# Agent attention with a squared-ReLU feed-forward: four transposes per group in one set, values weighed a block ahead over seven groups, second weights decoded in two parts

## The chip, the core and the metric

The kernel runs on one core of one Trainium2 chip. The time is the device time of one execution in microseconds (us). Three executions of the kernel before took 1960.69, 1955.43 and 1959.62 us; the median is 1959.62.

The engines are named as the profile names them: PE is the matrix engine (PEld its weight loads), DVE the vector engine, ACT the scalar (activation) engine, POOL the GpSimd engine, SP the engine that issues the DMAs.

## The reference

```python
B, N, C = 4, 12480, 128; n_agents = 49; d_ff = 2048
def sm(a, b):                         # softmax over the last axis
    s = (a @ b.transpose(0, 2, 1)) / sqrt(C); s = s - s.max(-1, keepdims=True)
    e = exp(s); return e / (e.sum(-1, keepdims=True) + 1e-9)
x = sm(q, agents) @ (sm(agents, k) @ v)        # 4 x 12480 x 128
h = maximum(x.reshape(-1, 128) @ w_in, 0)      # w_in 128 x 2048, as 64-bit floats
return (h * h) @ w_out                         # w_out 2048 x 128, as 64-bit floats
```

All is float32 but the two weight matrices, which arrive as 64-bit floats and are decoded on the chip from their two 32-bit words (`raw[:, :, 0]` low, `raw[:, :, 1]` high).

## The kernel before

**Tokens.** A group is 960 tokens (eight tiles of 120), so each of the four batches has 13 groups and there are 52. A group has two halves of 480 tokens and 16 slots; half 0 has slots 0 to 7, half 1 slots 8 to 15. A slot covers 256 of the 2048 hidden columns for one half. The loop works in pairs of slots (8 pairs a group): `first` issues the products into `h` for both slots, `second` the products into `o` for the slots four earlier (`LAG = 4`, so two pairs earlier). `o` is one PSUM bank; it is summed over a half's eight slots and then scaled out of PSUM by DVE as `ob` (`out`). With the lag, the sum of half 0 begins in the third pair of its group (slot 4) and that of half 1 in the seventh (slot 12); in each of these places the first product into `o` must wait until DVE has read the sum before.

**One pair.** PE: four products `h<-w,aw_hi`, four short ones `h<-x,aw_ex` side by side, then twelve into `o`. ACT: `r` twice (ReLU) and `g_hi` (the square, 1920 columns). DVE: `gg`, `h` (in place in PSUM) and `g_lo`. POOL: two `g_lo`. `gg` has two buffers (`GB`), `h` three, `g_lo` four.

**Attention beside it.** While batch b is fed forward, a generator (`background`) makes the attention of batch b+1: 13 blocks of `scores` (keys), `maxima`, 13 blocks of `values`, then `tables`, which makes `aw_hi` and `aw_ex`, the product of the attention with `w_in`. `step` advances it to its next `yield`, whose number is a price in slots; a `yield 0` stands ahead of a product and is passed only in the slots of `SPOTS`. Products of this kind go to one PSUM bank (`psa`), and `share` puts them between the first products of `o`: as a rule eight in a slot, four where `many` is set. Where a sum into `o` begins, some may stand ahead of its first product.

**Queries.** For each group, `queries` makes the scores of its 960 tokens (8 products), the softmax, transposes of its weights (4 in all), and, by 28 small DMAs over SP, the tiles `w` and `x` of both halves. It too is advanced at fixed slots: DMA of `qt` in slot 4 two groups ahead, scores in slot 14 (half of them put in slot 14, half in slot 0), softmax in slots 1 to 3, two transposes in slot 8, two in slot 12.

**Prologue.** Before group 0 the attention of batch 0 runs alone (13 key blocks, 13 value blocks, `tables`) with the decode of `w_in`. `w_out` is loaded in eight chunks (`load_w_out`) and decoded in group 0, behind the first `aw_half` (`issue_after(state[0]["cut"])`): the eight maxima, a power of two, then eight times `decode_w_out`.

**Order.** The instructions are put into each engine's queue by a scheduler; `queued` and `issue_after` fix that one comes behind another on its engine. An engine takes its queue in order.

Of the kernel before, what the change touches and what calls it, by code (L numbers as in the profile page):

```python
# [18 lines left out]
P = 128  # L19
# [16 lines left out]
PAIRED = (0, 2, 1, 3, 4, 6, 5, 7)  # L36
SPOTS = (1, 2, 3, 5)
# [3 lines left out]
def agent_attention_relu2(ctx: ExitStack, tc: tile.TileContext, qT, kT, v, agT, w_in, w_out, outT):  # L41
# [54 lines left out]
    def decoded(raw, up=None):  # L96
        low, high = raw[:, :, 0], raw[:, :, 1]
# [7 lines left out]
        nc.vector.tensor_scalar(t, t, 0x07FFFFFF, 3, op0=ALU.bitwise_and, op1=ALU.logical_shift_left)  # L105
        nc.vector.scalar_tensor_tensor(
            out=t, in0=high, scalar=0xC0000000, in1=t, op0=ALU.bitwise_and, op1=ALU.bitwise_or
        )
        if up is not None:
            nc.vector.tensor_scalar_mul(t.bitcast(F32), t.bitcast(F32), up)  # L110
# [3 lines left out]
        nc.vector.scalar_tensor_tensor(out=rest, in0=low, scalar=2.0**-52, in1=rest, op0=ALU.mult, op1=ALU.mult)  # L114
        return t.bitcast(F32), rest

    def load_w_in(dec, n):
        cs = slice(n * WCH, (n + 1) * WCH)
        t, rest = decoded(load_raw(w_in.bitcast(U32)[:, 2 * n * WCH : 2 * (n + 1) * WCH]))
        nc.gpsimd.tensor_add(win[:, cs], t, rest)  # L120
        nc.vector.reduce_max(top[:, n : n + 1], win[:, cs], axis=AX.X, apply_absolute_value=True)
# [10 lines left out]
    def powers_of_w_out():  # L132
# [11 lines left out]
        queued(nc.tensor.matmul, nc.tensor, ps[:, :1], ones, e.bitcast(F32), start=True, stop=True)  # L144
# [55 lines left out]
    def scores(b, i, kt):  # L200
# [7 lines left out]
        yield 1.2  # L208
# [29 lines left out]
    def halves(out, x, n, eng):  # L238

        nc.scalar.copy(out[:, :, :n], x)  # L240
        yield 1
        last[eng] = eng.tensor_sub(out[:, :, n:], x, out[:, :, :n].bitcast(F32))

    def values(b, i, vt, whole, eng):
# [6 lines left out]
        if not whole:  # L251
# [4 lines left out]
            yield 1  # L256
# [5 lines left out]
        yield 1  # L262
# [3 lines left out]
        else:  # L266
            e = small.tile([TP, NT, R], F32R, name="e2", bufs=2)
            yield from halves(e, d, NA, eng)
            vt = vs
        yield 0  # L270
# [9 lines left out]
        if i == 0 and not whole:  # L280
            nc.vector.tensor_copy(st["av"], pv[:R, :W])
        else:
            nc.vector.tensor_add(st["av"][:R, :W], st["av"][:R, :W], pv[:R, :W])

    def tables(b):
# [3 lines left out]
        nc.vector.tensor_add(x, st["av"][:, : C + 1], st["av"][:, C + 1 :])  # L289
# [68 lines left out]
    def queries(g, early=None):  # L358
# [29 lines left out]
        pairs = e.rearrange("p (j u h) a -> p j u (h a)", j=2, h=2)  # L388
        for j in range(2):
            yield  # L390
            pt = bank()
            w = qp.tile([P, G], F32R, name=f"w{j}", bufs=2)
            x = qp.tile([P, G], F16, name=f"x{j}", bufs=2)
            weights[g].append((w, x))
            if early:
# [10 lines left out]
                for t in range(NQ):  # L406
                    nc.sync.dma_start(x[t * 32 : t * 32 + NL, :], half[SP:, :])
                continue
            put([
                product(  # L410
                    pt[:K2, u * TP : (u + 1) * TP], pairs[:, j, u], ident[:TP, :TP],
                    is_transpose=True, start=True, stop=True,
                )
                for u in range(2)
            ])
            yield
            y = qp.tile([K2, 2 * TP], F32, name="y", bufs=1)
            nc.scalar.copy(y, pt[:K2, : 2 * TP])
            hi = qp.tile([K2, 2 * TP], F32R, name="ph", bufs=2)
            lo = qp.tile([K2, 2 * TP], F32R, name="pl", bufs=1)  # L420
            half = qp.tile([K2, 2 * TP], F16, name="half", bufs=2)
            nc.gpsimd.tensor_copy(hi, y)  # L422
            nc.gpsimd.tensor_sub(lo, y, hi.bitcast(F32))  # L423
            nc.gpsimd.tensor_copy(half, hi.bitcast(F32))
            yield
            for h in range(2):
                cs, at = slice(2 * h * TP, 2 * (h + 1) * TP), h * NA
                nc.sync.dma_start(w[:NA, cs].bitcast(F32), hi[at : at + NA, :].bitcast(F32))
                nc.sync.dma_start(w[NA:K2, cs].bitcast(F32), lo[at : at + NA, :].bitcast(F32))
                nc.sync.dma_start(w[K2:, cs].bitcast(F32), hi[at : at + SP, :].bitcast(F32))  # L430
                for t in range(NQ):
                    nc.sync.dma_start(x[t * 32 : t * 32 + NL, cs], half[at + SP : at + NA, :])
# [16 lines left out]
    def first(k):  # L449
# [23 lines left out]
        for n in range(2):  # L473
            nc.gpsimd.tensor_sub(lo[:, n, :], gg[:, n, :], hi[:, 0, n, :].bitcast(F32))  # L474
# [56 lines left out]
    def background(b):  # L531

        kt = load_keys(b, 0, kv, "kt")
        for i in range(NB):
            nxt = load_keys(b, i + 1, kv, "kt") if i + 1 < NB else load_values(b, 0, kv, "vt")
            yield from scores(b, i, kt)
            yield
# [3 lines left out]
        vt = kt  # L541
        for i in range(NB):
            nxt = load_values(b, i + 1, kv, "vt") if i + 1 < NB else None
            yield from values(b, i, vt, False, nc.gpsimd)
            yield
            vt = nxt
        yield from tables(b)

    def step(gen):

        with ExitStack() as es:
            for ins in behind:
# [17 lines left out]
    with tc.tile_pool(name="pre", bufs=PRE) as pre:  # L570
# [17 lines left out]
        for i in range(NB):  # L588
            run(values(0, i, vts[i], i not in HALVED, nc.vector))
            if i + PRE < NB:  # L590
                vts.append(load_values(0, i + PRE, pre, "ahead"))
            if i >= QAT:
                next(q0, None)
        run(q0)
        with tc.issue_after(last[nc.sync].ins):
            raws = [load_w_out(n) for n in range(NW)]
# [7 lines left out]
    ahead = queries(1)  # L604
    later = None
    for k in range(total + LAG):
        if k < total:
# [9 lines left out]
            for _ in range(2):  # L617
                if want == "end" or (want == 0 and (c % 2 or c // 2 not in (SPOTS if g else (3, 4)))) or credit < want or fill:
                    break
                credit -= want  # L620
# [6 lines left out]
            if g + 1 < B * NB:  # L627
                if c == 0:
                    if g == 0:
                        step(ahead)  # L630
                    else:
                        ahead = later
                if c in ((4, 5, 6, 7, 10, 11, 12, 13, 14) if g == 0 else (1, 2, 3, 8, 9, 10, 12, 13, 14)):
                    step(ahead)
                if g == 0 and c == 11:
                    step(ahead)
            if g + 2 < B * NB:
                if c == 4:
                    later = queries(g + 2)
                    step(later)  # L640
                if c == 14:
                    step(later)
            many[0] = c in (0, 14)
# [3 lines left out]
            if k == 0:  # L647
                with tc.issue_after(state[0]["cut"]):
                    most_of_w_out(raws)
                    scale_out.extend(powers_of_w_out())  # L650
                    nc.vector.tensor_mul(state[0]["down"], state[0]["down"], scale_out[1])
                    for n in range(NW):
                        decode_w_out(n, raws[n], scale_out[0])
        if k % 2 == 0:
            ready = second(k - LAG) if k >= LAG else flush()
            next(begun, None)
# [36 lines left out]
```

## Time and profile before

| | |
|---|---|
| median of three | 1959.62 us |
| the profiled execution | 1961.76 us |
| its span, first to last instruction | 1960.0 us |
| busy: PE, ACT, DVE, POOL | 96%, 86%, 85%, 70% of the span |
| mean granted clock of PE | 0.983 of full speed |

One execution was recorded. A busy row counts an instruction from its start to its end; idle time ahead of an instruction of over 0.15 us is shown in square brackets with what ended it. The granted clock of a stretch is a share of full speed (2.4 GHz); it changes between 1.0 and 0.5 (1.2 GHz).

### The profile page before, as it was taken

To read this page: it belongs to the slowest core of one execution; us is meant where nothing else is said; L and a number is where in the kernel's file an instruction comes from. 1 tells how busy PE (TensorE), PEld (TensorE's weight loads), DVE (VectorE), ACT (ScalarE), POOL (GpSimd) and SP (SyncE) were. 2 spreads that over 40 slices of the span, in tenths; PEclk is the share of its full clock that TensorE was granted. 3 is DMA by queue.
4 is the path that set the end of the run, shared out by engine and by line. 5 is a ranking of instruction groups with operands and counts; after the bars stand their busy time and mean duration, and the time that the engine had idled before them with its cause. 6 is when DMAs were issued, how large, how long until landed. Compare 5 with 4: busy or idle time off the path is not lost.

```text
span 1960.0 us, 32252 instructions
## 1 busy us (share of the span) xinstructions
PE 1888.3 (96%) x10778; PEld 1408.3 (72%) x10778; DVE 1670.2 (85%) x1936; ACT 1676.7 (86%) x1664; POOL 1374.7 (70%) x1441
## 2 busy tenths in 40 slices
PE   7679999999999999999999999999999999999998
PEld 7457777777677777776677776777677777777776
DVE  6778888889988788889988888888988888888887
ACT  3567799998888889998888888998889898989897
POOL 2565579996665679996666558997667676666675
PEclk8779999999999999999999999999999999999999
DMA  9323313232113223222112322321111111111110
GB/s 292 108 78 100 98 50 96 80 87 68 41 51 109 85 64 96 81 82 67 42 61 67 95 79 59 84 82 40 47 61 40 61 40 61 39 57 43 50 41 32
DMA packets 91209, 142.91 MB, mean 73 GB/s; under 512 B 28174, under 2 KB 69986, under 8 KB 91042
## 3 DMA queue, kind: packets, MB, share of 16 engines
q1 hardware_dynamic: 91042, 140.84, 24.1%
q8 instruction: 86, 1.41, 0.3%
q14 instruction: 81, 0.66, 0.1%
HBM read 81.17 MB, written 25.56 MB: 54 GB/s over the span
## 4 chain that ended last, share of the span: by engine, by line
PE 75%; DVE 11%; ACT 4%; DMA 3%; issue 3%; POOL 1%; SPq 1%; POOLq 0%; DVEq 0%; ACTq 0%
PE o L445 45%; PE h L445 20%; PE psa L445 9%; DVE gg L445 3%; ACT r L445 3%; DVE g_lo L445 2%; DVE h L445 2%; DMA raw<-in_w_in 1%; ACT g_hi L445 1%; DVE ob L445 1%; DMA ahead<-in_v 1%; POOL g_lo L474 1%; DVE z L379 1%; DVE m L372 1%; DMA ahead<-in_kT 0%
## 5 line engine op out<-in xcount | busy, mean ns | idle before, releaser
L474 POOL TENSOR_TENSOR g_lo<-gg,g_hi 128x480 f16<-128x480 f32 x832 | 996.9, 1220 | 382.3 <-ACT g_hi L445 189.4
L445 ACT ACTIVATE r<-h 128x960 f32<-128x960 f32 x832 | 763.0, 968 | 163.3 <-PE h L445 108.4
L445 ACT ACTIVATE g_hi<-r 128x1920 fp32r<-128x1920 f32 x416 | 755.2, 1815 | 25.2 <-ACT r L445 0.7
L445 DVE TENSOR_TENSOR g_lo<-h,g_hi 128x960 f16<-128x960 f32 x416 | 479.8, 1153 | 120.2 <-ACT g_hi L445 102.1
L445 PE MATMUL o<-g_hi,wo_hi 128*128 128x480 f32 x1664 | 574.0, 426 | 0.0
L445 DVE TENSOR_TENSOR gg<-r,h 128x960 f32<-128x960 f32 x416 | 479.3, 1152 | 104.8 <-ACT r L445 91.7
L445 PE MATMUL o<-g_lo,wo_half 128*128 128x480 f16 x1664 | 511.8, 370 | 25.8 <-DVE ob L445 16.8
L445 PE MATMUL o<-g_hi,wo_lo 128*128 128x480 f32 x1664 | 500.2, 382 | 0.4 <-POOL wo_lo L161 0.4
L445 DVE TENSOR_TENSOR h<-r,h 128x960 f32<-128x960 f32 x416 | 480.2, 1154 | 0.2
L445 PE MATMUL h<-w,aw_hi 128*128 128x480 f32 x1664 | 435.9, 382 | 8.0 <-DMA aw_hi<-aw_lo 3.9
L445 PEld LDWEIGHTS h<-w,aw_hi 128*128 128x128 f32 x1664 | 313.6, 190 | 64.7 <-DVE gg L445 10.9
L445 PEld LDWEIGHTS o<-g_hi,wo_hi 128*128 128x128 f32 x1664 | 317.2, 191 | 56.0 <-issue 1.3
L445 PEld LDWEIGHTS o<-g_hi,wo_lo 128*128 128x128 f32 x1664 | 315.4, 190 | 50.7 <-POOL wo_lo L161 1.2
L445 PEld LDWEIGHTS <-wo_half 128*128 128x128 f16 x1664 | 182.8, 114 | 163.3 <-issue 100.1
L445 PE MATMUL h<-x,aw_ex 19*128 19x480 f16 x1664 | 162.3, 373 | 0.8 <-DMA x<-half 0.7
L445 PEld LDWEIGHTS <-aw_ex 19*128 19x128 f16 x1664 | 42.4, 91 | 140.4 <-issue 136.4
L445 PEld LDWEIGHTS psa<-ag,qt 128*120 128x120 f32 x816 | 128.8, 187 | 10.4 <-DMA qt<-in_qT 4.4
L445 PE MATMUL psa<-ag,qt 128*120 128x49 f32 x816 | 118.1, 248 | 3.9 <-DMA qt<-in_qT 3.9
L382 POOL TENSOR_TENSOR e<-e,z 120x392 f32<-120x392 f32 x52 | 44.1, 849 | 79.0 <-PE h L445 42.3
L257 POOL TENSOR_TENSOR vs<-vt,vs 120x1024 fp32r<-120x1024 f32 x39 | 86.1, 2207 | 12.3 <-ACT vs L255 12.2
L445 PEld LDWEIGHTS psa<-ag,kt 128*120 128x120 f32 x624 | 80.6, 184 | 5.7 <-PE h L445 1.8
L423 POOL TENSOR_TENSOR pl<-y,ph 98x240 fp32r<-98x240 f32 x102 | 72.2, 708 | 12.0 <-POOL ph L422 3.9
(150 smaller groups left out, 1166.3 us busy)
## 6 DMA issues: line engine op xcount, KB each, us to landing
qt<-in_qT SPq DMA_DIRECT2D x52, 480.0 KB
out_T<-ob SPq DMA_DIRECT2D x104, 240.0 KB
vt<-in_v SPq DMA_DIRECT2D x39, 483.8 KB
kt<-in_kT SPq DMA_DIRECT2D x39, 480.0 KB
x<-half SPq DMA_DIRECT2D x816, 8.9 KB
w<-ph SPq DMA_DIRECT2D x204, 45.9 KB
w<-pl SPq DMA_DIRECT2D x204, 45.9 KB
ahead<-in_v SPq DMA_DIRECT2D x13, 483.8 KB
```

Of the source, the lines that this page charges most:

```text
L257: last[nc.gpsimd] = nc.gpsimd.tensor_sub(vs[:, :, C + 1 : 2 * C + 1], vt[:, :, :C], vs[:, :, :C].bitcast(F32))
L372: nc.vector.reduce_max(m, sv, axis=AX.X)
L379: nc.vector.reduce_sum(z, e, axis=AX.X)
L382: nc.gpsimd.tensor_mul(e, e, z.broadcast_to([TP, NT, NA]))
L423: nc.gpsimd.tensor_sub(lo, y, hi.bitcast(F32))
L445: ins = issue(*args, **kw)
L474: nc.gpsimd.tensor_sub(lo[:, n, :], gg[:, n, :], hi[:, 0, n, :].bitcast(F32))
```

## The change

1. **Queries.** The four transposes of a group are put as one set in slot 4, into one PSUM bank (98 rows x 480), and `w` and `x` of both halves are then made with one copy (`y`), one rounded part, one remainder (in place in `y`) and 14 DMAs with rows twice as long. `PAIRED` gives the order of the tiles that this needs. The scores are put in slots 10 and 12, four in each.
2. **Values.** `values` is split into `weighed` and `gathered`; `background` weighs block i+1 before it issues the products of block i. Yields of 1 become `PACE = 1.4`, and `SPOTS` is (0, 1, 3, 4, 7) in all groups. ACT, DVE and POOL instructions of a step are put behind those of the pair before last (`marks`).
3. **Second weights.** The eight maxima and the first part of the decode (`magnitudes`, in place in `raw`) are put behind the ninth value block of the prologue (`OPEN = 8`), the power of two behind `x`; the scaling, the remainders and the split follow behind the first `aw_half` as before. The DMA of `qt` for group 1 is issued ahead of the loads of `w_out`.

```diff
-PAIRED = (0, 2, 1, 3, 4, 6, 5, 7)
-SPOTS = (1, 2, 3, 5)
+PAIRED = (0, 2, 4, 6, 1, 3, 5, 7)
+OPEN = 8
+SPOTS = (0, 1, 3, 4, 7)
+PACE = 1.4
...
     def decode_w_out(n, raw, up):
         c = slice(n * WCH // C, (n + 1) * WCH // C)
-        t, rest = decoded(raw, up)
+        t = raw[:, :, 1].bitcast(F32)
+        nc.vector.tensor_scalar_mul(t, t, up)
+        rest = remainders(raw, raw[:, :, 1])
...
+        pairs = e.rearrange("p (u h) a -> p u (h a)", h=2)
+        yield
+        pt = bank()
+        put([
+            product(
+                pt[:K2, u * TP : (u + 1) * TP], pairs[:, u], ident[:TP, :TP], is_transpose=True, start=True, stop=True
+            )
+            for u in range(NT // 2)
+        ])
+        yield
+        y = qp.tile([K2, G], F32, name="y", bufs=1)
+        nc.scalar.copy(y, pt[:K2, :G])
+        hi = qp.tile([K2, G], F32R, name="ph", bufs=1)
+        half = qp.tile([K2, G], F16, name="half", bufs=1)
+        nc.gpsimd.tensor_copy(hi, y)
+        nc.gpsimd.tensor_sub(y.bitcast(F32R), y, hi.bitcast(F32))
+        nc.gpsimd.tensor_copy(half, hi.bitcast(F32))
...
+        vt = load_values(b, 1, kv, "vt")
+        ready = yield from weighed(b, 0, kt, False, nc.gpsimd)
         for i in range(NB):
-            nxt = load_values(b, i + 1, kv, "vt") if i + 1 < NB else None
-            yield from values(b, i, vt, False, nc.gpsimd)
-            yield
-            vt = nxt
+            yield PACE
+            nxt = load_values(b, i + 2, kv, "vt") if i + 2 < NB else None
+            more = (yield from weighed(b, i + 1, vt, False, nc.gpsimd)) if i + 1 < NB else None
+            yield from gathered(b, i, *ready)
+            vt, ready = nxt, more
...
+    with tc.issue_after(opened):
+        most_of_w_out(raws)
+        for raw in raws:
+            magnitudes(raw, raw[:, :, 1])
+    with tc.issue_after(state[0]["x"]):
+        scale_out.extend(powers_of_w_out())
+    with tc.issue_after(state[0]["cut"]):
+        nc.vector.tensor_mul(state[0]["down"], state[0]["down"], scale_out[1])
+        for n in range(NW):
+            decode_w_out(n, raws[n], scale_out[0])
...
-                if c in ((4, 5, 6, 7, 10, 11, 12, 13, 14) if g == 0 else (1, 2, 3, 8, 9, 10, 12, 13, 14)):
+                if c in (4, 5, 6) or (g == 0 and c < 4):
                     step(ahead)
...
-                if c == 4:
+                if c == 2:
                     later = queries(g + 2)
+                if c in (2, 10, 13, 14, 15):
                     step(later)
-            many[0] = c in (0, 14)
+            many[0] = c in (10, 12)
```

**Three places in the order of the engines.** The first is PE in the third pair of group 12 (groups counted from 0), where a sum into `o` begins; `psa<-ident,e` is a transpose, `o<-g_lo,wo_half` the first product of the sum. Before:

```order
L445 MATMUL h<-x_5653,aw_ex 128x480
L445 LDWEIGHTS wo_half
L445 MATMUL o<-g_lo,wo_half 128x480
L445 LDWEIGHTS wo_half
L445 MATMUL o<-g_lo,wo_half 128x480
```

and now:

```order
L463 MATMUL h<-x_5330,aw_ex 128x480
L463 MATMUL psa<-ident,e 98x120 x2
L463 LDWEIGHTS wo_half
L463 MATMUL o<-g_lo,wo_half 128x480
L463 MATMUL psa<-ident,e 98x120
L463 LDWEIGHTS wo_half
L463 MATMUL o<-g_lo,wo_half 128x480
L463 MATMUL psa<-ident,e 98x120
```

Two transposes now stand between the last product into `h` and the first into `o`. In the seventh pair, where before two transposes stood in this place, now two score products do.

DVE at the same place, from the pair ahead on. Before:

```order
L379 TENSOR_REDUCE z<-e 120x8
L445 TENSOR_TENSOR gg<-r,h 128x960
L380 TENSOR_SCALAR z<-z 120x8
L445 TENSOR_TENSOR h<-r,h 128x2x480
L381 RECIPROCAL z<-z 120x8
L445 TENSOR_SCALAR ob<-o,down 128x480
```

and now:

```order
L463 TENSOR_TENSOR g_lo<-h,g_hi 128x960
L463 TENSOR_TENSOR gg<-r,h 128x960
L463 TENSOR_TENSOR h<-r,h 128x2x480
L463 TENSOR_SCALAR ob<-o,down 128x480
L463 TENSOR_TENSOR g_lo<-h,g_hi 128x960
```

The softmax of the queries (`m`, `e`, `z`), which stood in the two pairs ahead of `ob`, now stands at the end of the group before and the start of this one.

The second place is ACT where group 0 begins. Before:

```order
L339 ACTIVATE aw_hi<-h,rl 98x512 x4
L445 ACTIVATE r<-h 128x960 x2
L445 ACTIVATE g_hi<-r 128x1920
L445 ACTIVATE r<-h 128x960
L158 CAST wo_hi<-t 128x256
L159 CAST wo_half<-t 128x256
```

and now, the last of sixteen such casts with the first `r` behind them:

```order
L167 CAST wo_half<-raw 128x256
L166 CAST wo_hi<-raw 128x256
L354 ACTIVATE aw_hi<-h,rl 98x512
L167 CAST wo_half<-raw 128x256
L463 ACTIVATE r<-h 128x960 x2
L463 ACTIVATE g_hi<-r 128x1920
```

All sixteen casts of `w_out` now stand ahead of the first `r` of the feed-forward; before, they were spread over its first six pairs.

The third place is POOL in group 7, among the values. Before, one stretch of three pairs:

```order
L474 TENSOR_TENSOR g_lo<-gg,g_hi 128x480 x2
L257 TENSOR_TENSOR vs<-vt,vs 120x8x128
L242 TENSOR_TENSOR e_3946<-d,e_3946 120x8x49
L422 CAST ph<-y 98x240
L474 TENSOR_TENSOR g_lo<-gg,g_hi 128x480 x2
L249 TENSOR_TENSOR d<-s,mb 120x392
L474 TENSOR_TENSOR g_lo<-gg,g_hi 128x480 x2
L423 TENSOR_TENSOR pl<-y,ph 98x240
L424 CAST half<-ph 98x240
```

and now:

```order
L397 TENSOR_TENSOR e<-e,z 120x392
L257 TENSOR_TENSOR d<-s,mb 120x392
L261 MEMSET vs 120x8
L262 MEMSET vs 120x8
L265 TENSOR_TENSOR vs<-vt,vs 120x8x128
L492 TENSOR_TENSOR g_lo<-gg,g_hi 128x480 x4
L250 TENSOR_TENSOR e_3747<-d,e_3747 120x8x49
L437 CAST ph<-y 98x480
L492 TENSOR_TENSOR g_lo<-gg,g_hi 128x480 x2
L438 TENSOR_TENSOR y<-y,ph 98x480
L439 CAST half<-ph 98x480
```

Two blocks of values a group instead of three; what is not `g_lo` comes in fewer and larger lumps.

## Rows read from the trace of the kernel before

**Rows 1.** The page, sections 1 and 2: busy time, share of the span and instructions of each engine; the granted clock in 40 equal slices, in tenths.

```profile
PE 1888.3 (96%) x10778; PEld 1408.3 (72%) x10778; DVE 1670.2 (85%) x1936; ACT 1676.7 (86%) x1664; POOL 1374.7 (70%) x1441
...
PEclk8779999999999999999999999999999999999999
```

**Rows 2.** The waits of PE over the whole run: engine, tile and line, and what it waited for; us in total, times, longest.

```profile
PE o L445 <- DVE ob L445: 16.8, 27, 1.4
...
PE o L445 <- ACT wo_half L159: 8.1, 2, 5.0
PE psa L445 <- DVE m L221: 4.5, 2, 2.3
...
PE o L445 <- POOL g_lo L474: 0.5, 1, 0.5
```

**Rows 3.** Stretches: from:to, length, busy us (instructions) of PE, PEld, DVE, ACT, POOL, then granted clock, DMA share, GB/s. In order: the end of the prologue; group 0; group 44 (queries alone); group 14 (four key blocks); group 6 (three value blocks); group 8 (three multiplied, one prepared); group 16 (one key block, the maxima, one value block); eight us within it.

```profile
66.00:86.00 20.00, 13.02 (x71) 8.12 (x69) 11.35 (x40) 5.22 (x9) 3.05 (x7) 0.86 0.09 24
86.00:146.00 60.00, 43.07 (x183) 30.15 (x184) 48.83 (x81) 38.70 (x52) 40.16 (x41) 0.71 0.30 87
1689.40:1722.50 33.10, 32.49 (x183) 23.73 (x182) 29.40 (x31) 29.86 (x28) 22.60 (x24) 1.00 0.16 50
619.00:657.70 38.70, 38.70 (x248) 30.76 (x247) 31.63 (x36) 31.39 (x32) 22.75 (x24) 1.00 0.30 94
335.70:371.90 36.20, 36.15 (x206) 26.67 (x205) 30.30 (x35) 34.44 (x37) 35.11 (x40) 1.00 0.31 86
408.10:443.10 35.00, 34.98 (x202) 26.13 (x201) 30.37 (x36) 31.98 (x31) 31.03 (x36) 1.00 0.27 77
696.60:736.80 40.20, 37.52 (x209) 27.99 (x209) 32.15 (x37) 33.70 (x37) 30.21 (x34) 0.96 0.20 63
706.00:714.00 8.00, 6.55 (x26) 4.65 (x27) 5.61 (x8) 3.82 (x5) 3.35 (x4) 0.79 0.08 31
```

**Rows 4.** The timeline of PE in group 44: start, us, operation [idle ahead, what ended it]. The first three rows are its second and third pairs, the last two its seventh.

```profile
1692.32 0.38 PE L445 MATMUL h<-x,aw_ex 19*128 19x480 f16 x4
...
1696.15 0.38 PE L445 MATMUL h<-x,aw_ex 19*128 19x480 f16 x4
1697.14 0.97 PE L445 MATMUL o<-g_lo,wo_half 128*128 128x480 f16 x4 [0.61 <-DVE ob L445]
...
1712.66 0.41 PE L445 MATMUL psa<-ident,e 120*98 120x120 f32 x2
1712.96 0.97 PE L445 MATMUL o<-g_lo,wo_half 128*128 128x480 f16 x4
```

**Rows 5.** The timeline of DVE in the same group, at the first place where `ob` is read.

```profile
1696.42 0.67 DVE L445 TENSOR_SCALAR ob<-o,down 128x480 f32<-128x480 f32 x1
```

**Rows 6.** Instructions of ACT in group 6 by line: shapes, count | busy us, mean ns | idle ahead.

```profile
L255 ACT CAST vs<-vt 120x1024 fp32r<-120x1024 f32 x3 | 3.1, 1036 | 0.0
L240 ACT CAST e<-d 120x392 fp32r<-120x392 f32 x3 | 1.6, 521 | 0.0
L263 ACT ACTIVATE d<-d 120x392 f32<-120x392 f32 x3 | 1.6, 519 | 0.0
```

**Rows 7.** Instructions of POOL in group 6, same columns.

```profile
L474 POOL TENSOR_TENSOR g_lo<-gg,g_hi 128x480 f16<-128x480 f32 x18 | 21.6, 1218 | 0.0
L257 POOL TENSOR_TENSOR vs<-vt,vs 120x1024 fp32r<-120x1024 f32 x3 | 6.6, 2202 | 1.1 <-ACT vs L255 1.1
...
L423 POOL TENSOR_TENSOR pl<-y,ph 98x240 fp32r<-98x240 f32 x2 | 1.4, 690 | 0.0
...
L422 POOL CAST ph<-y 98x240 fp32r<-98x240 f32 x2 | 0.8, 380 | 0.0
```

**Rows 8.** The timeline of DVE in the prologue and in group 0: its first and last row there are the first `gg` of group 0 and of group 1; between them the steps of the decode of `w_out` (L105 shift, L101 limits, L106 join, L110 scaling, L113 and L114 remainder).

```profile
58.17 2.18 DVE L113 TENSOR_SCALAR rest<-t 128x256 uint32<-128x256 uint32 x1
...
85.92 1.13 DVE L445 TENSOR_TENSOR gg<-r,h 128x960 f32<-128x960 f32 x1
...
115.67 0.29 DVE L105 TENSOR_SCALAR t<-t 128x256 uint32<-128x256 uint32 x1
115.88 0.29 DVE L101 TENSOR_SCALAR t<-t 128x256 f32<-128x256 f32 x1
116.08 0.42 DVE L106 SCALAR_TENSOR_TENSOR t<-raw,t 128x256 uint32<-128x256 uint32 x1
...
116.61 0.35 DVE L110 TENSOR_SCALAR t<-t,up_out 128x256 f32<-128x256 f32 x1
...
117.21 0.29 DVE L113 TENSOR_SCALAR rest<-t 128x256 uint32<-128x256 uint32 x1
...
117.68 0.42 DVE L114 SCALAR_TENSOR_TENSOR rest<-raw,rest 128x256 f32<-128x256 uint32 x1
...
122.17 1.46 DVE L106 SCALAR_TENSOR_TENSOR t<-raw,t 128x256 uint32<-128x256 uint32 x1
...
145.88 1.16 DVE L445 TENSOR_TENSOR gg<-r,h 128x960 f32<-128x960 f32 x1 [0.84 <-ACT r L445]
```

**Rows 9.** Instructions of ACT between 60 and 150 us by line: the casts of `w_out` to its upper part.

```profile
L158 ACT CAST wo_hi<-t 128x256 fp32r<-128x256 f32 x8 | 3.2, 403 | 9.2 <-DVE t L110 9.2
```

**Rows 10.** Instructions of POOL between 75 and 146 us by line: the split of `w_out`.

```profile
L160 POOL TENSOR_TENSOR t<-t,wo_hi 128x256 f32<-128x256 f32 x8 | 6.8, 852 | 7.0 <-DVE t L110 2.4 <-ACT wo_half L159 1.9 <-DVE rest L113 1.8
L161 POOL TENSOR_TENSOR wo_lo<-t,rest 128x256 fp32r<-128x256 f32 x8 | 6.0, 753 | 0.3
```

More of the change, by code (lines that the diff above doesn't have):

```diff
@@ L240, in halves, with weighed @@
         nc.scalar.copy(out[:, :, :n], x)
-        yield 1
+        yield PACE
         last[eng] = eng.tensor_sub(out[:, :, n:], x, out[:, :, :n].bitcast(F32))
-    def values(b, i, vt, whole, eng):
+    def weighed(b, i, vt, whole, eng):
         st = state[b]
@@ L269, in values, with gathered @@
             vt = vs
+        return e, vt, R, W, whole
+    def gathered(b, i, e, vt, R, W, whole):
+        st = state[b]
         yield 0
@@ L282, in values @@
         else:
-            nc.vector.tensor_add(st["av"][:R, :W], st["av"][:R, :W], pv[:R, :W])
+            st["sum"] = nc.vector.tensor_add(st["av"][:R, :W], st["av"][:R, :W], pv[:R, :W]).ins
+    def values(b, i, vt, whole, eng):
+        yield from gathered(b, i, *(yield from weighed(b, i, vt, whole, eng)))
     def tables(b):
@@ L387, in queries @@
             yield from halves(pp, e, NA, nc.gpsimd)
-        pairs = e.rearrange("p (j u h) a -> p j u (h a)", j=2, h=2)
-        for j in range(2):
-            yield
[L391 to L395, printed above, removed]
+        if early:
+            for j in range(2):
+                yield
+                pt = bank()
+                w = qp.tile([P, G], F32R, name=f"w{j}", bufs=2)
+                x = qp.tile([P, G], F16, name=f"x{j}", bufs=2)
+                weights[g].append((w, x))
                 put([
@@ L407, in queries @@
                     nc.sync.dma_start(x[t * 32 : t * 32 + NL, :], half[SP:, :])
[L408 to L432, printed above, removed]
+            return
@@ new lines, in queries @@
+        nc.gpsimd.tensor_copy(hi, y)
+        nc.gpsimd.tensor_sub(y.bitcast(F32R), y, hi.bitcast(F32))
+        nc.gpsimd.tensor_copy(half, hi.bitcast(F32))
+        yield
+        for j in range(2):
+            w = qp.tile([P, G], F32R, name=f"w{j}", bufs=2)
+            x = qp.tile([P, G], F16, name=f"x{j}", bufs=2)
+            weights[g].append((w, x))
+            at = j * NA
+            nc.sync.dma_start(w[:NA, :].bitcast(F32), hi[at : at + NA, :].bitcast(F32))
+            nc.sync.dma_start(w[K2:, :].bitcast(F32), hi[at : at + SP, :].bitcast(F32))
+            for t in range(NQ):
+                nc.sync.dma_start(x[t * 32 : t * 32 + NL, :], half[at + SP : at + NA, :])
+            nc.sync.dma_start(w[NA:K2, :].bitcast(F32), y[at : at + NA, :])
@@ L595, in agent_attention_relu2 @@
         with tc.issue_after(last[nc.sync].ins):
+            ahead = queries(1)
+            next(ahead)
             raws = [load_w_out(n) for n in range(NW)]
@@ L603, in agent_attention_relu2 @@
     many = [False]
-    ahead = queries(1)
     later = None
@@ L617, in agent_attention_relu2 @@
             for _ in range(2):
-                if want == "end" or (want == 0 and (c % 2 or c // 2 not in (SPOTS if g else (3, 4)))) or credit < want or fill:
+                if want == "end" or (want == 0 and (c % 2 or c // 2 not in SPOTS)) or credit < want or fill:
                     break
-                credit -= want
+                credit = credit - want if want else 0.0
                 want = step(todo)
@@ L627, in agent_attention_relu2 @@
             if g + 1 < B * NB:
[L628 to L632, printed above, removed]
[L633 to L635 removed]
+                if c == 0 and g:
+                    ahead = later
+                if c in (4, 5, 6) or (g == 0 and c < 4):
                     step(ahead)
             if g + 2 < B * NB:
[L638 removed]
+                if c == 2:
                     later = queries(g + 2)
+                if c in (2, 10, 13, 14, 15):
                     step(later)
[L641 to L643 removed]
+            many[0] = c in (10, 12)
             if k % 2 == 0:
@@ L646, in agent_attention_relu2 @@
                 next(begun)
[L647 to L653, printed above, removed]
         if k % 2 == 0:
             ready = second(k - LAG) if k >= LAG else flush()
+            marks.append([chain[nc.scalar], chain[nc.vector], chain[nc.gpsimd]])
             next(begun, None)
```

47 lines of the change are left out of this document (28 added, 19 removed).

## Prediction

> **What bounds the kernel now.** I read the page's busy shares first: PE 96%, ACT 86, DVE 85, POOL 70, the granted clock full but for the first four of forty slices [rows 1]. So I take PE as the bound and count a change where PE idles or runs at half clock. The waits of PE come next: the long list begins with `o` waiting for DVE's `ob`, 16.8 us in 27 waits; then `wo_half`, 8.1 us, and the maxima `m`, 4.5 us in two; `g_lo` hardly at all, 0.5 [rows 2]. Last I cut the run into groups [rows 3]. A plain group (44) lasts 33.10 us with PE busy 32.49: 0.61 us is lost. Four key blocks make 38.70 with PE full, so a key block costs PE (38.7−32.5)/4 = 1.55 us. Group 8, with three values multiplied and one prepared, is PE-full too: (35.0−32.5)/3 = 0.83 us a block. Group 6, which prepares three, lasts 36.2, 1.2 us more, with ACT busy 34.4 and POOL 35.1. Group 16, which takes the maxima, lasts 40.2 where PE's own work is 32.5+1.55+0.83 = 34.9; in eight us of it PE is busy 6.55 and the granted clock is 0.79. Group 0 lasts 60.0 with PE busy 43.1 at 0.71.
>
> **The change, part by part.** The sums are against the profiled execution, 1961.8 us, which is 2.1 above the median; I subtract 2.1 at the end.
>
> *Queries.* In group 44 the first `o` product of the third pair starts 0.61 us late, released by `ob`, while in the seventh pair two transposes fill the same place and PE has no gap [rows 4]. `ob` starts at 1696.42, right behind the softmax's `z`, and takes 0.67 [rows 5]. Now two transposes stand in the first place and two scores in the second, and the softmax is no longer ahead of `ob` on DVE. Two transposes hold PE for 1712.96−1712.66 = 0.30 us, half of the gap; the other half should come from DVE, which has no softmax left ahead of `ob` there. Of the 16.8 us I take 14. Bounds: 0 (`ob` moves with PE) and −16.8. The softmax now ends groups and begins them, off PE's path as long as its results are wanted pairs later. Its costs on ACT, DVE and the queues are not more than before: one `y` copy for two, three POOL operations of twice the length for six, 14 DMAs for 28. I put them at 0, since PE covers them: ACT and POOL have 3.2 and 10.5 us idle in a plain group [rows 3].
>
> *Maxima.* With the blocks spread otherwise, `m` is now made a pair or more ahead of the product that needs it. Group 16's loss is 40.2−34.9 = 5.3: 40.2−37.5 = 2.7 of idle PE, of which 2.25 are this wait, and 37.5−34.9 = 2.6 more of busy PE, the slower clock in the stretch behind it (0.79) [rows 2, 3]. Rows 2 count two such waits; the second I price alike, 10.6, and take 10. The bounds are 0 (the wait comes elsewhere) and −10.6. The third batch change shows no such wait.
>
> *Values.* There are 39 blocks in the loop, three batches of 13. Now three a group, then two. Group 6's excess of 1.2 us is 0.4 a block, 15.6 in all. For a block taken out of a group ACT loses 1.04+0.52+0.52 = 2.08 us [rows 6], POOL at least 2.2 for `vs` [rows 7]. So a group of two has PE 32.5+2×0.83 = 34.2, ACT 34.4−2.1 = 32.4, and POOL about 35.1−2.2−`d`, `e` and memsets (taken as 2) = 31. Group 8 has ACT 32.0 and POOL 31.0 of 35.0 and no excess: shares of 91 and 89%. The new group has 95 and 90%: by POOL it is like group 8, by ACT like group 6 (95 and 97%). I take half: −8. Bounds: −15.6, and above nothing, if all of the 20 groups that now hold values lose what group 6 loses: 20×1.2−15.6 = +8.
>
> *Second weights.* Group 0 lasts from 85.92 to 145.88 [rows 8], 60.0−33.1−1.55 = 25.4 us more than a plain group with one key block. 17 of its 60 us PE idles; the slower clock costs 43.07−32.49−1.55 = 9.0. ACT's casts of `w_out` waited 9.2 us for the scaling `t` on DVE [rows 9], and PE 8.1 for `wo_half` [rows 2]. Now the first part of the decode stands in the prologue, where from 66 to 86 DVE is busy 11.35 of 20 [rows 3]. It gets limits, shift and join of six more chunks, 6×(0.29+0.29+0.42) = 6.0, eight scalings 2.8, and the remainders of four chunks ahead of the first `gg`, 4×(0.29+0.42) = 2.8 [rows 8]: 22.9 in 20, so the first `gg` comes 2.9 later, about 88.8. ACT has 16 casts, 6.4 us at 0.40 [rows 9], before the first `r`; it was busy 5.2 of those 20, so this is hidden. In group 0 I keep 9 of the 17 idle us (its first pairs still run at the pace of `r`, `g_hi` and the last remainders) and 3.5 of the 9.0 of slower clock: 12.5 of excess in place of 25.4, −13 and +2.9 for the late start. The cover that opens takes two more key blocks into it, 3.1. Sum −13. Bounds: −25.4, all of the excess; and above nothing, if the split's 6.8+6.0 us on POOL [rows 10] come one behind another ahead of PE: +12.8.
>
> What speaks against this part is a meeting of DVE and POOL. The same `L106` that took 0.42 us at 116.08 took 1.46 at 122.17, and `L113` 2.18 at 58.17 where it takes 0.29 at 117.21 [rows 8]; the new place is the one where POOL prepares the values. The Trainium skill, SBUF — State Buffer, section "SBUF: two separate sides", says that the port pair which DVE and GpSimd share is an exclusive lock, held for a whole instruction, against DVE operations with two SBUF inputs or in a two-port mode; the two rows agree with that. By that rule every decode step beside a POOL instruction waits for its end; that would take this part's gain away, which is the first rival.
>
> *Sum.* −14−10−8−13 = −45: 1916.8 profiled, 1914.7 for the median; I say **1915**.
>
> **Rivals.**
> (1) *The decode only moves.* DVE meets POOL in the prologue as in the two slow rows, the first `gg` comes 10 to 15 us later instead of 2.9, and this part gives 0: 1915+13 = 1928. For it: the rows of 1.46 and 2.18 us; POOL's `vs` among the ninth to the thirteenth value block. Against it: POOL is busy only 3.05 of the 20 us from 66 on [rows 3].
> (2) *Values get no lighter.* ACT at 95% or larger lumps on POOL (all of a block's work in one piece, 2.2 us of `vs` alone [rows 7]) keep the excess in 20 groups: +8 in place of −8, 1931. Against it: group 8.
> (3) *The gap at `ob` stays*: the two transposes fill only 0.30 of 0.61 us and `ob` itself waits for PE's last product into `o`, so PE still idles; −14 becomes 0: 1929. This is the case of a change that does not do what it says. Against it: the seventh pair, where the same filling left no gap.
> (4) *The other side: POOL's lump between two `g_lo`.* The rounded part, the remainder and the half-precision copy of the queries now cover 480 columns: twice 0.38 and 0.69 [rows 7] with the copy like the first, 2.9 us in one or two lumps in each of 52 groups, where `g_lo` follows at 1.22 a piece. If `g_lo` then comes later than its two pairs of lead, PE waits in every group. From 45/52 = 0.87 us a group the gains are gone; at 1.5 us it is −45+78 = +33: 1959.6+33 = 1993. Against it: POOL idles 10.5 us in a plain group, two pairs are 2×(1696.15−1692.32) = 7.7 us [rows 4], and PE waited for `g_lo` once in the whole run [rows 2].
>
> **How the numbers follow.** Forecast 0.58; rival 1 0.18; rival 2 0.10; rival 3 0.07; rival 4 0.05; the rest 0.02, more than one rival together, near 1945. The forecast's own range is 1903 to 1927: all of `ob` and the values' best (−10.4 more) below, half the gain of the decode and of the values (10.5 less) above, and 2 over at each end for the clock. The rivals 1 to 3 lie at 1928 to 1931, each with its own spread of some 7. Range 1898 to 1938, which leaves about 1 in 10 above and less below. A measurement of this kernel tells 0.3%, 6 us, from no change. Faster by that, below 1953.7: all of the forecast and rivals 1 to 3, and most of the rest: 0.92. Within it: a part of rival 4 near its turning point and of mishaps together: 0.04. Slower: the rest of rival 4, 0.04.
>
> **What would show it.** Right: plain groups at 32.5 instead of 33.1, and no `ob` among PE's waits; no `m` there and a full clock past the first groups; value groups with two blocks at 34.2 to 34.8; the first `gg` at 88 to 90 and group 1's at 130 to 135; `wo_half` gone from PE's waits. Wrong: decode rows of over 0.6 us in the prologue and a first `gg` beyond 95 (rival 1); value groups at 35.4 (rival 2); `ob` waits of 0.3 us in each group (rival 3); `g_lo` among PE's waits some fifty times (rival 4). A new wait of PE on the queries' `m` or `e`, now nearer to the ends of groups, would make it wrong in a way that I give no chance of its own.

## The result and the profile after

The changed kernel takes 1924.81 us (median of four, 1924.42 to 1926.35); the kernel before, beside it, 1959.55. The ratio is 0.9828, 95% interval 0.9811 to 0.9845: 1.7% faster, 34.7 us of the 45 that were forecast. The profiled execution, the slowest of the four, has a span of 1924.6 us. The page's busy shares and clock, against [rows 1], and PE's waits, against [rows 2]:

```profile
PE 1881.1 (98%) x10778; PEld 1403.1 (73%) x10778; DVE 1663.8 (86%) x1936; ACT 1681.0 (87%) x1613; POOL 1353.1 (70%) x1288
...
PEclk8789999999999999999999999999999999999999
```

```profile
PE o L463 <- DVE ob L463: 5.5, 20, 0.3
PE psa L463 <- POOL e L397: 4.7, 1, 4.7
PE h L463 <- DVE aw_lo L356: 4.0, 2, 2.1
PE h L463 <- issue: 3.2, 1, 3.2
...
PE o L463 <- POOL g_lo L492: 0.5, 1, 0.5
```

PE has as many instructions as before and 7 us less busy time; the rest of the gain is idle time. `ob` fell from 16.8 us to 5.5, `m` and `wo_half` are gone from the list; 4.7 us for the queries' `e` are new, and 4.0 for `aw_lo` stand where before 3.9 us went to the DMA of `aw_hi`. Stretches, columns as in [rows 3]: group 44 (queries alone), group 7 (two value blocks), group 0, the end of the prologue.

```profile
1659.30:1691.90 32.60, 32.60 (x182) 23.71 (x181) 29.41 (x33) 29.97 (x27) 22.25 (x21) 1.00 0.16 51
359.20:394.10 34.90, 34.62 (x197) 25.64 (x196) 30.35 (x33) 33.27 (x33) 30.25 (x31) 1.00 0.26 76
90.90:138.20 47.30, 39.28 (x217) 29.46 (x218) 36.56 (x47) 30.42 (x30) 29.55 (x30) 0.79 0.36 115
66.00:86.00 20.00, 14.56 (x77) 9.59 (x75) 18.66 (x74) 9.61 (x26) 5.53 (x6) 0.91 0.08 21
```

A plain group is full at 32.6 us. A value group is not: PE 34.62 of 34.90. At the end of the prologue DVE is now busy 18.66 of the 20 us where it had 11.35, and group 0 ends at 138.2 in place of 145.9 though it begins 5.0 later.

Cut at the ends of batches (by DVE's first `gg` of groups 1, 13, 26 and 39, and the last `ob`), the two traces differ by −7.7 us up to group 1, −6.1 in groups 1 to 12, −6.6 and −6.9 in the two middle batches, −7.5 in the last: −34.8 in all.

Where `ob` is read, in the third pair of a plain group; the changed kernel's DVE and PE (compare [rows 4, 5]):

```profile
1664.15 1.16 DVE L463 TENSOR_TENSOR h<-r,h 128x960 f32<-128x960 f32 x1
...
1664.39 1.02 PE L463 MATMUL h<-w,aw_hi 128*128 128x480 f32 x4
1665.22 0.71 DVE L463 TENSOR_SCALAR ob<-o,down 128x480 f32<-128x480 f32 x1
...
1665.66 0.41 PE L463 MATMUL psa<-ident,e 120*98 120x120 f32 x2
...
1665.98 0.36 PE L463 MATMUL o<-g_lo,wo_half 128*128 128x480 f16 x1
```

And the same place in group 7, a value group:

```profile
363.03 0.52 ACT L248 CAST e<-d 120x392 fp32r<-120x392 f32 x1
363.44 0.98 ACT L463 ACTIVATE r<-h 128x960 f32<-128x960 f32 x1
...
364.31 1.03 PE L463 MATMUL h<-w,aw_hi 128*128 128x480 f32 x4
364.45 1.16 DVE L463 TENSOR_TENSOR h<-r,h 128x960 f32<-128x960 f32 x1
...
365.52 0.71 DVE L463 TENSOR_SCALAR ob<-o,down 128x480 f32<-128x480 f32 x1
365.59 0.41 PE L463 MATMUL psa<-ident,e 120*98 120x120 f32 x2
...
366.28 0.36 PE L463 MATMUL o<-g_lo,wo_half 128*128 128x480 f16 x1 [0.28 <-DVE ob L463]
```

Take PE's first product of the pair as the zero. In the plain group `ob` starts at 0.83 and ends as the two transposes end: no gap. In the value group it starts at 1.21, as late as before the change (1696.42 to PE's 1695.19: 1.23), and the transposes cover only a part: 0.28 us are left, in 17 value groups. (The other three of the 20 waits, 0.23 us each, stand in the last two groups, where there are no more products to fill with.) The trace also shows what `ob` comes late behind: ACT has a value block's `d` ahead of the first `r` of the pair and its `e` between the two `r`; the second `r` ends at 364.42, and DVE's `h`, ahead of `ob`, starts at 364.45. All 17 places have this order and these distances. In the plain group the two `r` stand one behind the other, and DVE doesn't wait for them. So the gap went by two means, and the value groups have one of them.

### The profile page after: what moved, and what is told of

It is laid out like the page before. It is cut to its first block, busy times and chain, and to the rows that moved or that the text cites. A ratio compares the mean times of both kernels' runs of the same rounds, so it can differ in the third digit from the quotient of the medians.

```text
span 1924.6 us, 31151 instructions
## 1 busy us (share of the span) xinstructions
PE 1881.1 (98%) x10778; PEld 1403.1 (73%) x10778; DVE 1663.8 (86%) x1936; ACT 1681.0 (87%) x1613; POOL 1353.1 (70%) x1288
## 4 chain that ended last, share of the span: by engine, by line
PE 87%; ACT 5%; DVE 4%; issue 2%; DMA 2%; POOL 0%; POOLq 0%; DVEq 0%; ACTq 0%; SPq 0%
PE o L463 52%; PE h L463 23%; PE psa L463 11%; ACT r L463 3%; DMA ahead<-in_v 2%; PE h L193 2%; DVE ob L463 1%; ACT g_hi L463 1%; DVE gg L463 1%; DVE h L463 1%; ACT e L248 0%; ACT d L271 0%; DVE g_lo L463 0%; PE h L590 0%; DVE rest L116 0%
## 5 line engine op out<-in xcount | busy, mean ns | idle before, releaser
L463 PE MATMUL o<-g_lo,wo_half 128*128 128x480 f16 x1664 | 502.1, 369 | 6.5 <-DVE ob L463 5.5
L463 PEld LDWEIGHTS <-wo_half 128*128 128x128 f16 x1664 | 172.3, 113 | 128.7 <-issue 75.6
L463 PEld LDWEIGHTS psa<-ag,qt 128*120 128x120 f32 x816 | 122.9, 186 | 16.1 <-issue 11.1
L463 PE MATMUL psa<-ag,qt 128*120 128x49 f32 x816 | 122.9, 254 | 0.0
L463 PE MATMUL psa<-ag,kt 128*120 128x49 f32 x624 | 78.4, 258 | 0.6
```

The costliest lines, as they stand in the source:

```text
L463: ins = issue(*args, **kw)
```

## The experiments

Times are medians; the kernel before ran beside each set at 1959.4 to 1960.1. Four runs first split the change.

**Queries alone** (with the new slots of `SPOTS`, which the set of four needs, and the earlier DMA of `qt`):

```diff
-PAIRED = (0, 2, 1, 3, 4, 6, 5, 7)
-SPOTS = (1, 2, 3, 5)
+PAIRED = (0, 2, 4, 6, 1, 3, 5, 7)
+SPOTS = (0, 1, 3, 4, 7)
...
```

> The kernel before with the queries' part alone (one set of four transposes, scores in slots 10 and 12, the DMA of `qt` for group 1 ahead of the loads of `w_out`, and the five slots of `SPOTS`, which the new set needs). Theory A, the changed kernel's time is a ledger of what PE loses: the plain groups go from 33.1 to about 32.5, the `ob` waits of 16.8 us fall to under 4, some 10 us in all, 1948 to 1951. Rival: half of the gain comes from the blocks' new places, so that this part alone gives under 6, 1954 or more.

**Second weights alone** (item 3 of the change, without the earlier `qt`):

> The kernel before with the decode of the second weights in two parts alone. Theory A: the first `gg` comes 5 us later, the `wo_half` waits of 8.1 us go, group 0 is 12 us shorter: 1951 to 1953. Rival: the gain of group 0 came from the earlier DMA of `qt` and the queries' new places (PE's 3.9 us for `qt`), and the decode alone gives under 4: 1956 or more.

**Values alone** (`weighed`, `gathered`, `PACE`, `marks` and shorter yields behind the scores; old `SPOTS`):

> The kernel before with the values weighed a block ahead alone (PACE 1.4, marks; the old slots of SPOTS and the old crediting, since the old places of the queries leave no others). Theory A: a value block costs PE 1.02 us however many stand in a group, so spreading them gives nothing, and only the waits on the maxima and the slow clock behind them go where the blocks are moved: 1949 to 1955. Rival (the prediction's): besides, the excess of 0.4 us a block is halved, 8 us more: 1941 to 1946.

**All but the values** (queries and second weights as changed, three value blocks a group as before):

> The changed kernel with the old values (three a group, not a block ahead; queries and second weights as changed). Theory A: it lacks only the gain at the maxima, 8 to 11 us: 1933 to 1936 if it keeps the two `m` waits. Rival: the values' spreading is worth 8 more, 1941 or more.

Measured: queries 1938.45 (ratio 0.9896, 0.9881 to 0.9911), second weights 1948.03 (0.9941, 0.9926 to 0.9956), values 1964.14 (1.0020, 1.0009 to 1.0031), all but the values 1926.59 (1923.51 to 1930.87; 0.9834, 0.9818 to 0.9850). The first two add up: 21.0 + 11.4 = 32.4 for 32.8 together. The values' part alone costs 4.7 us, and on top of the others it gives 1.8, which this measurement can't tell from nothing. Queries and second weights did better than expected, the values alone worse than both theories, and the run with all but the values better than both: it had no `m` waits to keep. Its trace has one odd wait instead:

```profile
PE psa L454 <- DVE x L295: 4.0, 2, 3.7
```

The 3.7 us stand in group 20, which lasts 40.3 us at a clock of 0.96; group 33, with the same products, lasts 35.0. Without this one wait the run would come out at some 1921 to 1922, an estimate from that one trace, so even the 1.8 us aren't shown to come from the values.

Where the rest comes from, the waits of PE say; first with the values alone, then with the queries alone:

```profile
PE o L453 <- DVE ob L453: 15.5, 36, 0.6
...
PE psa L453 <- DVE m L222: 4.5, 2, 2.3
```

```profile
PE o L448 <- DVE ob L448: 1.7, 7, 0.3
```

The waits on the maxima stay when only the values are spread, and are gone when only the queries and their slots change. With the values alone `ob` waits come in 36 places, since the value groups join the plain ones.

**The maxima's place.** So the wait belonged to slot 4, where the transpose of the maxima stood ahead of the first `o` product. In the kernel before, only this:

```diff
         yield 2
+        apart[0] = True
         yield 0
+        apart[0] = False
...
```

While `apart` is set, slot 4 is left out (`or (apart[0] and c == 4)` in the test that holds a step back).

> The kernel before with one edit: the transpose of the maxima is kept out of slot 4, where it stood ahead of the first `o` product, and comes a pair later between two `o` products. Theory A: this place, and not the spreading of the values, made the two waits of 2.25 us for `m` and the half clock behind them; both go, group 16 falls from 40.2 to 35 to 36.5, and the run is 7 to 11 us faster, 1949 to 1953. Rival: the reduction of the maxima on DVE delays `ob` and `g_lo` wherever the transpose stands, so the wait turns into one on `ob`, and it stays within 3 us of 1959.5.

Measured 1954.19 (0.9974, 0.9962 to 0.9985): 5.9 us, short of theory A's 7 to 11. Group 16, then 17, in its trace:

```profile
694.90:730.20 35.30, 34.95 (x204) 26.20 (x203) 31.24 (x37) 32.15 (x34) 26.39 (x28) 1.00 0.19 62
730.20:766.80 36.60, 36.24 (x202) 25.97 (x201) 30.30 (x36) 34.86 (x37) 34.50 (x40) 1.00 0.28 79
```

Group 16 falls from 40.2 to 35.3 at a full clock, as theory A says, with a place and no spreading. But the two stretches don't hold the same work: one value block (about 1 us) now comes later, in group 21. And part is given back behind group 16 (group 17 goes from 35.9 to 36.6). The whole batch, groups 13 to 25, holds the same 2674 products in both; before, then in this run:

```profile
580.40:1051.90 471.50, 464.24 (x2674) 347.49 (x2673) 405.00 (x452) 416.63 (x410) 346.99 (x365) 1.00 0.25 74
```

```profile
578.80:1047.50 468.70, 464.01 (x2674) 346.11 (x2673) 403.24 (x451) 416.63 (x410) 347.20 (x365) 1.00 0.25 74
```

2.8 us in this batch, 3.0 in the next: that is the 5.9. In its group the wait with the slow clock behind it cost 5.3 us, but taking it away is worth only a little over half of that.

**No product ahead of the first `o`**, and **all four ahead**, in the changed kernel; the line that is replaced, and what the first run, then the second, has in its place:

```diff
-                due[0].append(due[3 if len(calls) > 2 else 1].pop())
...
+                due[:] = [[], [None], [None], [None, None]]
...
+                due[:] = [[None] * len(calls), [], [], []]
```

> The changed kernel with no product ahead of the first `o` product (the transposes and scores stand between the first products of `o` and behind). Theory A: both halves are needed, the 0.3 us of the two products and the earlier `ob`: without the first each of the 104 sums waits 0.25 to 0.4 us for `ob`, 26 to 40 us more, 1950 to 1965. Rival: it is enough that the softmax no longer stands ahead of `ob` on DVE: under 8 us more, 1933 or less.

> The changed kernel with all four transposes, and all four of the scores in slot 12, ahead of the first `o` product in place of two. Theory A: in the value groups `ob` comes 0.38 us later after the last `o` product than in a plain group, since DVE waits for ACT's `r`, and two products cover only 0.3 of it; four cover the rest: the 20 `ob` waits of 0.28 us go, 1918 to 1921, with plain groups as before at 32.55. Rival: PE loses the same time elsewhere, since `r` is late anyway: within 2 us of 1924.8.

Measured 1931.70 and 1927.02. The first is 6.9 us slower than the changed kernel, not 26 to 40: the rival was right about the time. Without a product ahead, plain group 44 of that trace has

```profile
1668.41 1.03 PE L463 MATMUL h<-w,aw_hi 128*128 128x480 f32 x4
1669.32 0.71 DVE L463 TENSOR_SCALAR ob<-o,down 128x480 f32<-128x480 f32 x1
...
1670.08 0.36 PE L463 MATMUL o<-g_lo,wo_half 128*128 128x480 f16 x1 [0.33 <-DVE ob L463]
```

a wait of 0.33 us in the first of the two places only, and lasts 32.8. So of the 0.5 to 0.6 us won in a plain group about 0.2 are the filling and the rest is the earlier `ob`: the softmax moved away. With all four ahead the `ob` waits go, as theory A says, but the value groups fall only to 34.85 (34.95 before) and the plain ones rise to 32.63: products that stand ahead of `o` don't stand between its products any more, which is a likely reason and wasn't tested. In time the run is 2.2 us slower; its rival had said within 2.

**The value groups.** Two runs ask why `ob` is late there. The rounding of `e` on DVE in place of ACT:

```diff
-        nc.scalar.copy(out[:, :, :n], x)
+        (nc.scalar.copy if alone[0] else nc.vector.tensor_copy)(out[:, :, :n], x)
```

> The changed kernel with the rounding of a value block's weights (0.52 us a block) on DVE in place of ACT inside the loop. Theory A: ACT's load of 95% in the value groups makes `r`, `gg` and `ob` late; with 1.04 us less in a group the 0.28 us waits go and the value groups fall from 34.95 to 34.6: 1917 to 1920. Rival: DVE is held up by POOL, or is the late one itself: the value groups stay or grow, 1925 to 1932.

Measured 1932.83, 8.0 us slower; the value groups grow to 35.2. The trace of its group 7:

```profile
362.63 0.81 DVE L248 CAST e<-d 120x392 fp32r<-120x392 f32 x1
...
363.36 1.14 DVE L463 TENSOR_TENSOR gg<-r,h 128x960 f32<-128x960 f32 x1
...
363.99 1.27 PE L463 MATMUL h<-w,aw_hi 128*128 128x480 f32 x4
...
366.25 0.36 PE L463 MATMUL o<-g_lo,wo_half 128*128 128x480 f16 x1 [0.33 <-DVE ob L463]
```

The 0.52 us taken from ACT became 0.81 on DVE, right ahead of `gg`, and `ob` is no earlier. This doesn't clear ACT, whose `d` and `e` around the first `r` stand ahead of the late `h` in the rows of group 7 above; it shows only that DVE is no place to move `e` to.

`ob` ahead of DVE's second `h`, with the transposes of group 1 late as in the next paragraph:

```diff
-            next(begun, None)
             if ready:
                 out(*ready)
+            next(begun, None)
```

> The kernel with the transposes of group 1's queries in slot 8 (1917.2), and `ob` ahead of DVE's second `h` in the pair where a sum ends. Theory A: in the value groups PE's 0.28 us come from `h` ahead of `ob`; `ob` starts as soon as the sum is done, the value groups fall from 34.95 to 34.6, and the run to 1909 to 1912. Rival: `ob` must wait for the sum's last product, `h` behind it comes 1 us later, and with it the PSUM buffer that PE's next `h` needs or `g_lo`: PE waits there in each group, 1917 to 1950.

Measured 1942.28, 25 us slower than without it. Stretches of its trace: group 6 (values), 44 (plain), 14 (keys).

```profile
320.70:355.20 34.50, 34.50 (x197) 25.55 (x196) 30.51 (x34) 33.26 (x33) 30.62 (x31) 1.00 0.28 77
1672.00:1705.20 33.20, 32.75 (x182) 23.44 (x181) 29.70 (x33) 29.91 (x27) 22.27 (x21) 1.00 0.15 49
605.30:647.50 42.20, 40.78 (x261) 32.27 (x261) 32.46 (x36) 31.76 (x32) 22.15 (x21) 1.00 0.32 97
```

Both theories hold, each in its groups. The value groups fall from 34.9 to 34.5 with PE full, so a late `h` ahead of `ob` is what kept PE there. Plain and key groups grow by 0.7 and 1.7. In a plain group PE now waits 0.45 us for `gg` (11.7 us in 26 waits over the run); in a key group it waits 0.9 and 0.6 us ahead of products into `psa`, and what ended most of these waits the profile doesn't tell. The edit in the value groups alone was not tried.

**Group 0.** Three runs on the new waits. The transposes of group 1's queries in slot 8 of group 0 in place of slot 4:

```diff
-                if c in (4, 5, 6) or (g == 0 and c < 4):
+                if c in ((0, 1, 2, 3, 8, 9, 10) if g == 0 else (4, 5, 6)):
...
```

> The changed kernel with the transposes of group 1's queries in slot 8 of group 0 in place of slot 4 (a key block takes slot 4). Theory A: PE's 4.7 us for `e` on POOL in group 0, at half clock, is a new wait that the set of transposes ahead of the first `o` product made; with it gone `o` starts when `g_lo` and the split weights are there: 3 to 6 us less, 1919 to 1922. Rival: something else of group 0 (the split on POOL, the remainders on DVE) ends at the same time, and it stays within 2 us of 1924.8.

And the scaling of the second weights behind the last `aw_half` (`st["cut"] = cut` for `setdefault`), without and with that edit:

> The changed kernel with the scaling of the second weights, and what follows it, behind the last `aw_half` in place of the first. Theory A: the scalings and remainders between the steps of `aw_lo` are what made the first `gg` 5 us later (PE's 4.0 us for `aw_lo`); it comes 3 to 5 us earlier, but the softmax of group 1's queries still holds the first `o`, so that only 0 to 3 us come out, 1922 to 1925. Rival: the delay of the prologue goes through to the end: 1919 to 1921.

> Both edits of group 0: transposes of group 1's queries in slot 8, and the scaling behind the last `aw_half`. Theory A: with the transposes gone, the first `o` waits for the split weights, which now come later: no better than the transposes' edit alone, 1917 to 1921. Rival: the decode is wholly covered there, and the 3 to 5 us of the earlier first `gg` come out: 1912 to 1915.

Measured 1917.17 (ratio to before 0.9780, 0.9765 to 0.9795), 1929.11 (1923.17 to 1929.86) and 1923.94. The late transposes gain 7.6 us on the changed kernel, a little more than theory A's 3 to 6. In the changed kernel PE stands idle in group 0 while the chain of group 1's softmax, queued on DVE and POOL among the remainders, ends:

```profile
99.46 0.59 PE L463 MATMUL h<-x,aw_ex 19*128 19x480 f16 x4
...
101.27 0.70 DVE L395 TENSOR_SCALAR z<-z 120x8 f32<-120x8 f32 x1
...
103.62 0.19 DVE L396 RECIPROCAL z<-z 120x8 f32<-120x8 f32 x1
...
103.89 0.84 POOL L397 TENSOR_TENSOR e<-e,z 120x392 f32<-120x392 f32 x1 [1.25 <-DVE z L396]
...
104.79 0.64 PE L463 MATMUL psa<-ident,e 120*98 120x120 f32 x2 [4.74 <-POOL e L397]
```

Group 0 of the run with late transposes:

```profile
88.70:129.10 40.40, 36.62 (x201) 26.54 (x202) 36.05 (x47) 29.92 (x29) 29.70 (x30) 0.85 0.39 121
```

40.4 us for 47.3, at a clock of 0.85 for 0.79. One key block of group 0 stands in group 3 there; at equal work, from the first `gg` of group 0 to that of group 5, it is 191.7 for 198.4, so that 6.7 us are gained. The scaling moved back lets the first `gg` come at 84.6 to 84.8 in place of 88.7 to 90.9, but group 0 then takes 50.4 to 50.5 (PE waits 4.3 to 4.5 us of it for the DMA of `aw_ex`), and with the late transposes the run loses 6.8 us, which neither theory had: there the decode does better in the prologue, even where it delays the first `gg`. Without them its runs spread over 6.7 us, and whether it gains or loses is not settled.

## Why the prediction was right, and where it was not

The direction and the range held; the forecast of −45 was 10 us too much. Term by term:

**Queries, −14.** Measured −11 to −12: PE's `ob` waits fell by 16.8−5.5 = 11.3, and the last batch, 13 groups without attention, by 7.5 = 13×0.58. The mechanism was as worked out, the filling and the earlier `ob`, but the halves were not even: about 0.2 us by filling, the rest by DVE. Of the 5.5 that are left, 4.8 stand in 17 value groups: rival 3, in a third of the groups, for which the prediction had allowed 2.8 us.

**Maxima, −10.** The cause was wrong, and the size is about half. "With the blocks spread otherwise" is not what did it: spreading alone left both waits. Slot 4 is no longer a spot, and this keeps the transpose out of the place ahead of the first `o`; the run that moves only it shows this, at 2.8 and 3.0 us a batch. In the changed kernel group 16 falls from 40.2 to 34.5, but a key block and the transpose have left it for other groups. Groups 13 to 16 together hold the same work in both kernels (13 key blocks, the maxima, one value block); before, then now:

```profile
580.40:736.80 156.40, 153.54 (x942) 120.19 (x941) 127.01 (x142) 127.77 (x130) 98.36 (x103) 0.99 0.28 86
```

```profile
566.60:720.20 153.60, 152.86 (x937) 118.39 (x936) 126.50 (x143) 128.56 (x125) 97.30 (x91) 1.00 0.30 91
```

2.8 us, and 2.6 in the third batch: −5.4.

**A term that was not in the sum.** The pairs of groups that make `tables` (21 and 22 before, 23 and 24 now, the same work again) got shorter:

```profile
881.30:952.40 71.10, 70.27 (x379) 49.39 (x378) 66.36 (x80) 61.79 (x61) 45.41 (x47) 1.00 0.19 58
```

```profile
929.90:998.90 69.00, 69.00 (x378) 49.53 (x377) 64.41 (x80) 61.86 (x59) 44.38 (x41) 1.00 0.17 53
```

About 2 us in each of three batches, −6. Part of it is two waits a batch of `psa` for `aw_lo` (2.2 us in all before, none now); why PE's own time there fell as well, no run asks. With the queries alone and their slots these groups get shorter too, with the values alone they don't, so this came with the new slots. That maxima and `tables` together come near the −10 that was forecast for the maxima is luck.

**Values, −8.** This is the step that failed: nothing was gained (1.8 at most, and 4.7 lost when alone). The term rested on 0.83 us of PE for a block, read from group 8 [rows 3] between two first `gg` of DVE. But DVE is late behind PE at the start of group 8 and not at its end: its first `gg` comes 3.59 us behind PE's first product there, and 2.53 us in group 9. Cut at PE's own first product, from the second pair of group 8 to the second pair of group 9 in the kernel before, the stretch with three value blocks begins and ends at

```profile
409.39 1.03 PE L445 MATMUL h<-w,aw_hi 128*128 128x480 f32 x4
...
445.05 1.03 PE L445 MATMUL h<-w,aw_hi 128*128 128x480 f32 x4
```

35.66 us apart, not 35.0: (35.66−32.5)/3 = 1.05 us a block. In the changed kernel a pair with a value block and the next one without start at

```profile
334.12 1.03 PE L463 MATMUL h<-w,aw_hi 128*128 128x480 f32 x4
338.95 1.03 PE L463 MATMUL h<-w,aw_hi 128*128 128x480 f32 x4
342.78 1.03 PE L463 MATMUL h<-w,aw_hi 128*128 128x480 f32 x4
```

4.83 and 3.83 apart: 1.00 us a block. With 1.0 the floor of a group with two blocks is 34.5, of one with three 35.5, so that group 6's excess was 0.7 and not 1.2 us, and the 0.4 us that each of the new value groups with an `ob` wait loses takes most of it back: 12 groups of three blocks at 0.7 = 8 against 17 groups of two at 0.4 = 7. Rival 2 came near: not by POOL's lumps, but by PE's price of a block and by the order of the engines: ACT's `d` and `e` ahead of the second `r`, which DVE's `h` waits for, and `h` ahead of `ob`. That `h` ahead of `ob` costs PE these 0.4 us is shown by the run that changes their order; that ACT makes `h` late is read from the trace alone.

**Second weights, −13.** Alone −11.4, and by its trace group 1 begins at 132.5 in place of 145.9, 13.4 earlier. In the changed kernel it is 7.7, and group 0 does three key blocks where it did one (2×1.55 = 3.1 us): −10.8. What is missing from the −13 is the wait on the queries' `e`, 4.7 us, which the prediction had as a possibility without a chance ("a new wait of PE on the queries' `m` or `e`"). The first `gg` came at 90.9 in this trace, 5.0 later and not 2.9; in the seven traces with this prologue it comes between 88.2 and 90.9, in the four with the old decode between 84.2 and 86.5, so that the delay is nearer to 4. The eight scalings stand between two steps of `aw_lo`, and the remainders beside POOL took longer than the 0.29 and 0.42 us of [rows 8]:

```profile
L116 DVE TENSOR_SCALAR rest<-raw 128x256 uint32<-128x256 uint32 x8 | 5.2, 655 | 0.0
L117 DVE SCALAR_TENSOR_TENSOR rest<-raw,rest 128x256 f32<-128x256 uint32 x9 | 4.7, 531 | 0.0
```

That is rival 1's mechanism, at a price of some 8×(0.655−0.29)+9×(0.531−0.42) = 3.9 us, about half of it ahead of the first `gg`, and not 13. The Trainium skill, SBUF — State Buffer, section "SBUF: two separate sides", says that the port pair which DVE and GpSimd share is an exclusive lock, held for a whole instruction, against DVE operations with two SBUF inputs or in a two-port mode; these rows agree, as does the `z` of 0.70 us at 101.27 (0.17 in the median of 52) beside POOL's two `raw`, 1.48 us from 101.17 on.

**Rival 4** did not occur: PE waits for `g_lo` once, 0.5 us, as before. **The sum** as measured: −10.8 (second weights, with the key blocks), −11.3 (queries), −5.4 (maxima), −6 (`tables`); what is left to the values, and to all that was not told apart, is −1: −34.8.

## What to carry to other kernels

Cut stretches at the bound engine's own first instruction: an interval between two marks of another engine holds that engine's drift too, and 0.66 us of it in one group made the price of a block a fifth too low. Compare stretches that hold the same work: a group that got 5 us shorter had passed a block on to another. Where a product must wait for an engine to empty its buffer, look at both sides, what the bound engine can do meanwhile and what stands ahead of the emptying instruction; and put nothing there that has a long chain of its own, as the maxima had before and the softmax of group 1 has now. A set of work that is placed well in the steady state can stand badly in the first round: moving the transposes of one group out of 52 was worth 7.6 us, and that kernel, 1917.2 us, is the fastest of these runs.

## What was not expected

Small waits of PE don't add up to the time: 0.33 us of idle at `ob` cost a plain group 0.2 us, and taking all of the value groups' 0.28 us away by products ahead gave 0.1. And the order on DVE of one 0.71 us instruction and one of 1.16 us is worth −0.4 us in a value group and +1.7 us in a key group.
